# Attention output made transposed in the steady slots of an attention and ReGLU kernel

## The chip, the cores and the metric

The kernel runs on one core of a Trainium2 chip, as one launch. The metric is the device time of one execution in microseconds, as the median of several runs. A core has a matrix engine (PE, with its weight loads shown apart as PEld), a vector engine (DVE), a scalar engine (ACT), a general engine (POOL, here also the one that issues the loads), a synchronising engine (SP, here the one that issues DMA transposes), and 16 DMA engines that all queues share. Matmul results land in PSUM, which has eight banks, numbered 0 to 7 here. A bank's slice is 512 fp32 numbers on each of 128 partitions.

## What is computed

Inputs are q, k, v of shape (8 batches, 8 heads, 576 positions, 64) and three FFN matrices of 512x1536, 512x1536 and 1536x512. The result is 4608 x 512 in fp32.

```python
q_d = q.reshape(B, H, Sd, 4, D).mean(axis=3)          # k_d, v_d alike
out_up = np.repeat(sm_attn(q_d, k_d, v_d), 4, axis=2)  # softmax attention, 144 positions
mask = np.abs(pos[:, None] - pos[None, :]) < 4
scores = np.where(mask, scale * q @ k.T, -1e9)
out_local = softmax(scores) @ v                        # 7 keys for each query
x = (out_up + out_local).transpose(0, 2, 1, 3).reshape(4608, 512)
out = (np.maximum(x @ w_gate, 0.0) * (x @ w_val)) @ w_out
```

## The kernel before

**Tiling.** Two heads make a head pair, `hp` 0 to 31, four for each batch. The 576 positions are cut into 6 query blocks of 96, and each meets a window of 128 keys that starts three positions earlier; the band mask zeroes what lies outside. Pooled positions are two blocks of 72. The FFN goes over the 4608 tokens in 9 chunks of 512, and over d_ff in 12 blocks of 128 (`jj`).

**Steps of a head pair.** `emit_load` issues the loads on POOL with a cast to fp16: q and k (`qk16`, a ring of 7), v windows of 128 rows (`vw`, ring of 7, with a column of ones behind the 64 values), and from pair `NVP` = 9 on a second view of v (`v4`). q and k are transposed to `qkT`, for pairs below `NTP` = 9 by matmuls on PE (`emit_qkT_pe`, which also gives the sums of four), from 9 on by a DMA transpose on SP (`emit_qkT`) with `emit_pool` on DVE for the sums. The pooled v (`vd`, ring of 2) is made by six matmuls (`emit_vd`) for pairs below 9, and by two additions on POOL (`emit_vd_pool`) from 9 on. `emit_s1` makes scores and exponentials: `ee`, keys on partitions, and `ed` for the pooled part. `emit_s2` multiplies with `ee` and `ed` as the weights and v (65 columns, the last one gives the denominators) as moving data; it takes 8 matmuls for the pooled and 12 for the local part, and DVE divides (two reciprocals, two multiplications) into `xo`, which has queries on partitions. The FFN needs x with features on partitions, so `xo` is transposed: pairs below `NXP` = 9 on PE (`emit_x_pe`, 8 matmuls, which also repeat and add the pooled part), later pairs by a DMA transpose on SP (`emit_xoT`) and an addition on DVE (`emit_xadd`).

**FFN.** `emit_h` makes one `jj` block: 4 + 4 matmuls of 512 columns into a pair of banks, a ReLU on ACT, a product on DVE (`gT`). `emit_y` makes 128 rows of the result from the twelve `gT` of the chunk before, 12 matmuls, a copy on ACT and a store issued by ACT.

**Order.** Everything is written in order by hand: each engine runs its instructions as the code issues them. A fill of four pairs (with dummy matmuls, `emit_warm`) is followed by 36 slots; slot s makes a third of a quarter of chunk s//4, that is three `emit_h`, one `emit_y` of the chunk before (from slot 4 on), and the attention of a pair. `s2` of a pair comes one slot after its `s1`. Slots 5 and 6 (`EXTRA`) hold two pairs each, so pair 31 has its `s1` in slot 25. Slots 27 to 35 are FFN alone. Chunk c needs the pairs up to 4c+3.

**The load queue.** POOL issues the loads of pair hp+4 at the head of pair hp, just ahead of `emit_vd_pool(hp)`, and then waits in order. An issue waits until the ring slot is free, and until the load eight issues earlier has landed (eight semaphores take turns). `emit_vd_pool(hp)` waits for its `v4` and for `s2` of pair hp-2, which read the same `vd` buffer. What stands behind it on POOL waits with it.

Of the kernel before, what the change touches and what calls it, by code (L numbers as in the profile page):

```python
# [57 lines left out]
def kernel(  # L58
# [26 lines left out]
    NXP = 9  # L85
    NVP = 9
    EXTRA = (5, 6)
    B0 = 1

# [30 lines left out]
    ee = ring(2, [128, 2, S + 32], FP16, "ee_")  # L120
# [3 lines left out]
    xoT = ring(3, [128, NB + 2, 96], FP16, "xoT_")  # L124
    xT = keep.tile([128, NPB, NTOK], FP16, name="xT")
    ps = psum.tile([128, 8, 512], FP32, name="ps")

    nc.vector.memset(zero_sb, 0.0)
    for t in vw:
        nc.vector.memset(t[:, :, :, 64], 1.0)  # L130
# [16 lines left out]
    def emit_load(hp):  # L147
# [18 lines left out]
        if off == 0:  # L166
            nc.gpsimd.dma_start(
                t[:, 1:, 0:64], _dap(v, base + NQ * D, [[D, 128], [NQ * D, n - 1], [1, D]])
            )
            nc.gpsimd.dma_start(t[3:128, 0, 0:64], _dap(v, 0, [[D, 125], [1, D]]))  # L170
            nc.gpsimd.dma_start(t[0:3, 0, 0:64], _dap(v, 0, [[D, 3], [1, D]]))
        elif b == B - 1 and hp % NPB == NPB - 1:
            nc.gpsimd.dma_start(
                t[:, 0 : n - 1, 0:64], _dap(v, base, [[D, 128], [NQ * D, n - 1], [1, D]])
            )
            last = base + (n - 1) * NQ * D
            nc.gpsimd.dma_start(t[0:99, n - 1, 0:64], _dap(v, last, [[D, 99], [1, D]]))
            nc.gpsimd.dma_start(t[99:128, n - 1, 0:64], _dap(v, last + 67 * D, [[D, 29], [1, D]]))
        else:
            nc.gpsimd.dma_start(t[:, :, 0:64], _dap(v, base, [[D, 128], [NQ * D, n], [1, D]]))  # L180
# [20 lines left out]
    def emit_qkT_pe(hp, b0):  # L201
        r, r4, r2 = hp % NL, hp % 4, hp % 2
        sv = qk16[r].rearrange("p i (h j d) -> p i h j d", h=2, d=64)
        for n in range(2 * NB):
            lo = 120 * (n % 4)
            for hh in range(2):
                nc.tensor.matmul(
                    out=ps[64 * hh : 64 * hh + 64, b0 + n // 4, lo : lo + 120],
                    lhsT=sv[:, n // NB, hh, n % NB, :],
                    rhs=eyesum_sb,  # L210
                    start=True,
                    stop=True,
                )
        big = qkT[r4][:, 0 : 2 * S].rearrange("p (b n t) -> p b n t", b=3, n=4)
        sml = qkd[r2].rearrange("p i t -> p (i t)").rearrange("p (b n t) -> p b n t", b=3, n=4)
        tv = ps[:, b0 : b0 + 3, 0:480].rearrange("p b (n t) -> p b n t", n=4)
        nc.scalar.copy(out=big[:, 0], in_=tv[:, 0, :, 0:96])
        nc.scalar.copy(out=sml[:, 0], in_=tv[:, 0, :, 96:120])
        nc.vector.tensor_copy(out=sml[:, 1:3], in_=tv[:, 1:3, :, 96:120])
        nc.vector.tensor_copy(out=big[:, 1:3], in_=tv[:, 1:3, :, 0:96])  # L220

    def emit_vd_pool(hp):
        t, m, o = v4[hp % NV4], v2[hp % 2], vd[hp % 2]
        if hp < NVP + 2:
            nc.gpsimd.memset(o[:, :, :, 64], 4.0)
# [14 lines left out]
    def emit_vd(hp, loc):  # L240
        t = vw[hp % NL]
        o = halves(loc)
        for c in range(2):
            for sig in range(3):
                nc.tensor.matmul(
                    out=o[:, c, :, :],
                    lhsT=pool_sb[:, sig, :],
                    rhs=t[:, :, 3 * c + sig, :],
                    start=(sig == 0),
                    stop=(sig == 2),  # L250
                )
        nc.scalar.copy(out=vd[hp % 2], in_=o[0:72])

    def emit_s1(hp):
        r4, r2 = hp % 4, hp % 2
        p0 = 2
# [21 lines left out]
        for g in range(2):  # L278
            o = ee[r2][:, :, 288 * g : 288 * g + 288]
            nc.scalar.activation(  # L280
                out=o, in_=ps[:, p0 + 2 * g : p0 + 2 * g + 2, 0:288], func=AF.Exp, scale=scale
# [4 lines left out]
                in1=_sap(masks_sb, (0, 128), 288 * g, [[0, 2], [1, 288]]),  # L286
# [9 lines left out]
    def emit_s2(hp, loc, pu):  # L296
# [3 lines left out]
        for hh in range(2):  # L300
            for tcx in range(2):
                for c in range(2):
# [4 lines left out]
                        rhs=vd[r2][:, c, hh, :],  # L307
# [30 lines left out]
    def emit_xoT(hp):  # L338
        x = xo[hp % 3]
        nc.sync.dma_start_transpose(out=xoT[hp % 3], in_=x.rearrange("p j c -> p (j c)"))  # L340

    def emit_xadd(hp):
        b, kk = hp // NPB, hp % NPB
        r3 = hp % 3
        nc.vector.tensor_tensor(
            out=xT[:, kk, b * S : (b + 1) * S].rearrange("p (c t f) -> p c t f", c=2, f=4),
            in0=xoT[r3][:, 0:NB, :].rearrange("p j t -> p (j t)").rearrange(
                "p (c t f) -> p c t f", c=2, f=4
            ),
            in1=_sap(xoT[r3], (0, 128), NB * 96, [[96, 2], [1, 72], [0, 4]]),  # L350
# [3 lines left out]
    def emit_x_pe(hp, pp, on_dve=False):  # L354
# [16 lines left out]
        if on_dve:  # L371
            nc.vector.tensor_copy(out=o, in_=pair(pp)[:, :, 0:288])
        else:
            nc.scalar.copy(out=o, in_=pair(pp)[:, :, 0:288])
# [3 lines left out]
    def emit_h(c, jj, pp):  # L378
# [10 lines left out]
        r1 = ffn.tile([128, TCH], FP16, name="r1", tag="r1")  # L389
        nc.scalar.activation(out=r1, in_=h1, func=AF.Relu)  # L390
        gt = gpool.tile([128, TCH], FP16, name="gT", tag="gT")
        nc.vector.tensor_tensor(out=gt, in0=r1, in1=h2, op=ALU.mult)
        gts[c, jj] = gt
# [54 lines left out]
    def emit_fill(hp):  # L448
        emit_in(hp + 4)
        emit_s1(hp)  # L450
# [5 lines left out]
        if hp < LEAD - 1:  # L456
            emit_qkT_pe(hp + 1, 2)
# [5 lines left out]
    def emit_att_head(hp, loc=7, pu=2):  # L463
        emit_in(hp + 4)
        if hp - 1 < NP:
            emit_s2(hp - 1, loc, pu)
            if hp - 1 >= NXP:
                emit_xoT(hp - 1)
        if NVP <= hp < NP:
            emit_vd_pool(hp)  # L470
        if NTP <= hp + 3 < NP:
            emit_qkT(hp + 3)

    def emit_att_mid(hp):
        if NTP <= hp + 1 < NP:
            emit_pool(hp + 1)
        if hp < NP:
            emit_s1(hp)

    def emit_slot(s, hp):  # L480
        c, jj = s // 4, 3 * (s % 4)
        if s == 0:
            emit_in(hp + 4)
            emit_qkT_pe(hp, 2)
# [3 lines left out]
            emit_h(c, jj, 3)  # L488
            emit_s1(hp)
        elif s == 4:  # L490
            emit_att_head(hp)
            emit_y(c - 1, s % 4, 6)
            emit_x_pe(hp - 1, 1, on_dve=True)
            emit_h(c, jj, 0)
            emit_att_mid(hp)
        else:
            emit_att_head(hp)
            emit_h(c, jj, 0)
            if hp - 1 < NXP:
                emit_x_pe(hp - 1, 3)  # L500
            emit_att_mid(hp)
            if s > 4:
                emit_y(c - 1, s % 4, 6)
        if NXP <= hp - 2 < NP:
            emit_xadd(hp - 2)
        emit_h(c, jj + 1, 0)
        if hp < NVP:
            emit_vd(hp, 7)
        if hp + 1 < NTP:
            emit_qkT_pe(hp + 1, 4)  # L510
        if s in EXTRA:
# [53 lines left out]
```

## Time and profile before

| what | value |
|---|---|
| median of 3 runs | 388.07 us (385.64 to 393.62) |
| the profiled execution, whole | 386.8 us |
| its span, first to last instruction | 384.7 us |
| PE busy | 360.3 us |
| DVE, ACT, POOL busy | 220.8, 154.3, 188.3 us |
| HBM read, written | 48.03 MB, 9.44 MB |

A line of the page for a group of instructions gives the program's line, engine, operation, what is written and read, and the count; then busy time, the mean duration of one, and the idle time before them with what ended it. Matmuls overlap in the pipeline, so the duration of one (388 ns for 512 columns) is longer than the distance from one to the next (216 ns: eight in 1.73 us); distances are what counts, and a row of the timeline gives the start of a group, so the distance to the start of the next row is what the group takes.

The order of time has three parts: up to 30 us the fill, up to about 293 us slots with attention, and from there to 381 us FFN alone.

### The profile page before, as it was taken

How to read it: one execution, taken by the hardware profiler on the slowest of the kernel's cores; microseconds unless marked ns; L12 is line 12 of the kernel's file. 1: busy time of each engine (PE TensorE's matmuls, PEld its weight loads, DVE VectorE, ACT ScalarE, POOL GpSimd, SP SyncE). 2: the span in 40 equal slices, each digit the busy share in tenths (PEclk: the TensorE clock that was granted, in tenths of full speed). 3: DMA queues.
4: the chain of work that ended last, by engine and by line, in shares of the span. 5: the costliest groups of instructions: out<-in, count | busy, mean ns of one | idle time of the engine just before them, and what ended most of it. 6: DMA issues, size and time to landing. Idle time of an engine off the chain costs nothing.

```text
span 384.7 us, 7154 instructions
## 1 busy us (share of the span) xinstructions
PE 360.3 (94%) x2834; PEld 181.1 (47%) x2834; DVE 220.8 (57%) x384; ACT 154.3 (40%) x276; POOL 188.3 (49%) x233
## 2 busy tenths in 40 slices
PE   7999997997779998999969999999999999999995
PEld 3665553453435453445434545545444444444442
DVE  2676765466859775877835897877764322222210
ACT  1665563442524443444414444444443332333321
POOL 8856574899678637965378789911000000000000
PEclk9999999898989998999978999999999999999999
DMA  9999999999999999999999999954222100010012
GB/s 128 146 155 178 155 179 169 173 156 155 142 169 137 159 137 137 124 175 129 124 148 132 164 173 183 165 99 88 60 43 54 55 29 27 27 56 28 29 47 89
DMA packets 191282, 45.41 MB, mean 118 GB/s; under 512 B 174257, under 2 KB 186513, under 8 KB 191249
## 3 DMA queue, kind: packets, MB, share of 16 engines
q0 software_dynamic: 140272, 23.86, 100.9%
q1 hardware_dynamic: 45776, 11.66, 28.1%
q10 hardware_dynamic: 5200, 9.44, 8.5%
q8 instruction: 22, 0.36, 0.5%
q14 instruction: 12, 0.09, 0.1%
HBM read 48.03 MB, written 9.44 MB: 149 GB/s over the span
## 4 chain that ended last, share of the span: by engine, by line
PE 53%; DMA 31%; POOL 12%; issue 3%; DVE 0%; ACT 0%; POOLq 0%; DVEq 0%
PE ps L382 31%; PE ps L398 17%; DMA qk_5_80<-in_k_dram 7%; DMA wv_sb<-in_moe_w_val_dram 6%; DMA qk_3_78<-in_k_dram 5%; DMA vw_90<-in_v_dram 4%; DMA wo_sb<-in_moe_w_out_dram 3%; DMA qk_4_79<-in_q_dram 3%; DMA vw_91<-in_v_dram 2%; DMA vw_93<-in_v_dram 2%; PE ps L314 2%; POOL v_1_88 L226 1%; PE ps L304 1%; PE ps L260 1%; PE ps L271 1%
## 5 line engine op out<-in xcount | busy, mean ns | idle before, releaser
L382 PE MATMUL ps<-xT,wg_sb 128*128 128x512 f16 x432 | 114.2, 388 | 0.0
L382 PE MATMUL ps<-xT,wv_sb 128*128 128x512 f16 x432 | 113.7, 387 | 0.0
L398 PE MATMUL ps<-wo_sb,gT 128*128 128x512 f16 x432 | 100.1, 382 | 3.6 <-DMA wo_sb<-in_moe_w_out_dram 3.4
L382 PEld LDWEIGHTS <-wv_sb 128*128 128x128 f16 x432 | 43.0, 100 | 53.4 <-issue 4.1
L398 PEld LDWEIGHTS <-gT 128*128 128x128 f16 x432 | 40.7, 98 | 51.8 <-issue 4.9
L382 PEld LDWEIGHTS <-wg_sb 128*128 128x128 f16 x432 | 40.2, 99 | 44.1 <-issue 2.2
L406 ACT COPY y_sb<-ps 128x512 f32<-128x512 f32 x36 | 21.1, 587 | 70.8 <-PE ps L398 70.8
L280 ACT ACTIVATE ee_102<-ps 128x576 f16<-128x576 f32 x32 | 19.3, 649 | 12.9 <-PE ps L271 12.9
L280 ACT ACTIVATE ee_103<-ps 128x576 f16<-128x576 f32 x32 | 19.1, 649 | 11.5 <-PE ps L271 11.5
L283 DVE TENSOR_TENSOR ee_103<-ee_103,cst_sb 128x576 f16<-128x576 f16 x32 | 20.7, 676 | 3.0 <-ACT ee_103 L280 2.6
L283 DVE TENSOR_TENSOR ee_102<-ee_102,cst_sb 128x576 f16<-128x576 f16 x32 | 18.1, 599 | 2.8 <-ACT ee_102 L280 2.5
L227 POOL TENSOR_TENSOR vd_107<-v_1_88 72x256 f16<-72x256 f32 x12 | 9.1, 760 | 14.5 <-PE ps L304 13.7
L444 PE MATMUL ps<-zero_sb 128*128 128x512 f16 x44 | 14.3, 449 | 1.3 <-DVE vw_89 L130 1.3
L304 PE MATMUL ps<-vd_106,ed_104 72*128 72x65 f16 x128 | 6.6, 195 | 8.8 <-POOL vd_106 L227 8.8
L227 POOL TENSOR_TENSOR vd_106<-v_0_87 72x256 f16<-72x256 f32 x11 | 8.2, 745 | 8.0 <-PE ps L304 7.2
L304 PEld LDWEIGHTS <-ed_104 72*128 72x128 f16 x128 | 6.0, 98 | 12.8 <-issue 9.7
L322 DVE RECIPROCAL rd<-ps 72x4 f32<-72x4 f32 x32 | 5.5, 173 | 10.8 <-PE ps L304 10.8
L331 DVE TENSOR_TENSOR xo_108<-ps,ru 96x768 f16<-96x768 f32 x11 | 10.5, 954 | 0.4
L331 DVE TENSOR_TENSOR xo_109<-ps,ru 96x768 f16<-96x768 f32 x11 | 10.5, 954 | 0.4
L289 ACT ACTIVATE ed_105<-ps 72x576 f16<-72x576 f32 x16 | 10.3, 645 | 0.0
L289 ACT ACTIVATE ed_104<-ps 72x576 f16<-72x576 f32 x16 | 10.3, 644 | 0.0
L304 PE MATMUL ps<-vd_107,ed_105 72*128 72x65 f16 x128 | 6.7, 196 | 3.8 <-POOL vd_107 L227 3.8
(393 smaller groups left out, 560.9 us busy)
## 6 DMA issues: line engine op xcount, KB each, us to landing
out_dram<-y_sb ACTq DMA_DIRECT2D x35, 256.0 KB, 2.2
wg_sb<-in_moe_w_gate_dram POOLq DMA_DIRECT2D x4, 384.0 KB, 10.7
wv_sb<-in_moe_w_val_dram POOLq DMA_DIRECT2D x4, 384.0 KB, 11.0
wo_sb<-in_moe_w_out_dram POOLq DMA_DIRECT2D x4, 384.0 KB, 9.8
vw_90<-in_v_dram POOLq DMA_DIRECT2D x5, 192.0 KB, 10.5
vw_91<-in_v_dram POOLq DMA_DIRECT2D x5, 192.0 KB, 8.4
vw_92<-in_v_dram POOLq DMA_DIRECT2D x5, 192.0 KB, 11.2
vw_89<-in_v_dram POOLq DMA_DIRECT2D x4, 192.0 KB, 11.0
```

What stands on the lines that cost most here:

```text
L227: nc.gpsimd.tensor_tensor(out=o[:, :, :, 0:64].rearrange("p c h d -> p h c d"), in0=m[:, :, 0:64].rearrange("p (h c) d -> p h c d", h=2), ...
L280: nc.scalar.activation(out=o, in_=ps[:, p0 + 2 * g : p0 + 2 * g + 2, 0:288], func=AF.Exp, scale=scale)
L283: nc.vector.tensor_tensor(out=o, in0=o, in1=_sap(masks_sb, (0, 128), 288 * g, [[0, 2], [1, 288]]), op=ALU.mult,)
L289: nc.scalar.activation(out=ed[r2][:, :, 0 : 2 * SD].rearrange("p h (c t) -> p c h t", c=2), in_=ps[0:72, p0 : p0 + 4, 288:432].rearrange(" ...
L304: nc.tensor.matmul(out=od[:, hh, tcx, :], lhsT=ed[r2][:, hh, s0 : s0 + 128], rhs=vd[r2][:, c, hh, :], start=(c == 0), stop=(c == 1),)
L314: nc.tensor.matmul(out=u[:, hh, j, :], lhsT=ee[r2][:, hh, NQ * j : NQ * j + 128], rhs=vw[hp % NL][:, hh, j, :], start=True, stop=True,)
L322: nc.vector.reciprocal(out=rd, in_=od[0:72, :, :, 64])
L331: nc.vector.tensor_tensor(out=x[:, 0:NB, :].rearrange("p j (h d) -> p h j d", h=2), in0=u[0:96, :, :, 0:64], in1=_sap(ru, (0, 96), 0, [[NB ...
L382: nc.tensor.matmul(out=h, lhsT=w[:, kk, bass.ts(jj, 128)], rhs=xT[:, kk, c * TCH : (c + 1) * TCH], start=(kk == 0), stop=(kk == 3),)
L398: nc.tensor.matmul(out=y_ps, lhsT=gts[c, jj][:, bass.ts(ty, 128)], rhs=wo_sb[:, jj, :], start=(jj == 0), stop=(jj == NJJ - 1),)
L406: nc.scalar.copy(out=y_sb, in_=y_ps)
L444: nc.tensor.matmul(out=ps[:, 7, :], lhsT=zero_sb[:, 0:128], rhs=zero_sb[:, 128:640], start=True, stop=True)
```

## The change

From slot 1 on, `emit_s2t` takes the place of `emit_s2` (which stays for pairs 0 to 3, with `emit_x_pe`). It swaps the operands: v (64 columns) is the weights, `ee` and `ed` are moving data, so the result has features on partitions, head 0 of the pair on partitions 0 to 63 and head 1 on 64 to 127. The denominators come from matmuls with a matrix of ones (of fours for pairs whose `vd` is a sum) as weights, so that they stand on the same partitions, in banks 4 and 5; the products are in banks 2 and 3. ACT makes the reciprocal as exp(-ln(den)), DVE multiplies and adds the pooled part, repeated four times, straight into `xT`. `emit_xoT`, `emit_xadd` and all `x` transposes of pairs 4 to 31 go.

Key windows have 112 rows instead of 128. `EXTRA` goes, so each slot has one pair and pair 31 has its `s1` in slot 27. `vd` is made by `emit_vd` for pairs up to 12, is a ring of three, and `emit_vd_pool(hp + 1)` stands ahead of the loads of pair hp+4. `emit_h` hands back its ReLU and product as a function `gate`: those of the last block of a slot are issued in the next slot, between the Ln and the Exp. Banks move: the scores use banks 4 to 7, the three `emit_h` banks 0-1, 2-3 and 6-7, `emit_y` bank 1. One table load for the activation functions is asked for at the start.

```diff
-    NXP = 9
-    NVP = 9
-    EXTRA = (5, 6)
+    NVP = 13
     B0 = 1
+    WK = 112
...
-    vw = ring(NL, [128, 2, NB, 65], FP16, "vw_")
+    vw = ring(NL, [WK, 2, NB, 65], FP16, "vw_")
...
-    vd = ring(2, [72, 2, 2, 65], FP16, "vd_")
+    vd = ring(3, [72, 2, 2, 65], FP16, "vd_")
...
+    nc.scalar.preload_act_table_set("natural_log_exp_and_others")
...
-            nc.gpsimd.dma_start(t[:, :, 0:64], _dap(v, base, [[D, 128], [NQ * D, n], [1, D]]))
+            nc.gpsimd.dma_start(t[:, :, 0:64], _dap(v, base, [[D, WK], [NQ * D, n], [1, D]]))
...
-    def emit_xoT(hp):
...
+    def emit_s2t(hp, between):
+        r2, b, kk = hp % 2, hp // NPB, hp % NPB
+        e, d, one = ee[r2], ed[r2], 64 * (hp >= NVP)
+        for g in range(2):
+            for hh in range(2):
+                nc.tensor.matmul(
+                    out=ps[64 * hh : 64 * hh + 64, 4 + g, 0:288],
+                    lhsT=ones_sb[0:WK, 0:64],
+                    rhs=e[:, hh, 288 * g : 288 * g + 288],
...
+            for c in range(2):
+                for hh in range(2):
+                    nc.tensor.matmul(
+                        out=ps[64 * hh : 64 * hh + 64, 4 + g, 288:360],
+                        lhsT=ones_sb[0:72, one : one + 64],
+                        rhs=d[:, hh, c * SD + 72 * g : c * SD + 72 * g + 72],
...
+        for g in range(2):
+            for j in range(3):
+                for hh in range(2):
+                    nc.tensor.matmul(
+                        out=ps[64 * hh : 64 * hh + 64, 2 + g, NQ * j : NQ * j + NQ],
+                        lhsT=vw[hp % NL][:, hh, 3 * g + j, 0:64],
+                        rhs=e[:, hh, 288 * g + NQ * j : 288 * g + NQ * j + NQ],
...
+            for c in range(2):
+                for hh in range(2):
+                    nc.tensor.matmul(
+                        out=ps[64 * hh : 64 * hh + 64, 2 + g, 288:360],
+                        lhsT=vd[hp % 3][:, c, hh, 0:64],
+                        rhs=d[:, hh, c * SD + 72 * g : c * SD + 72 * g + 72],
...
+        r, x = rden[r2], xn[r2]
+        nc.scalar.activation(out=r, in_=ps[:, 4:6, 0:360], func=AF.Ln)
+        between()
+        nc.scalar.activation(out=r, in_=r, func=AF.Exp, scale=-1.0)
+        nc.vector.tensor_tensor(out=x, in0=ps[:, 2:4, 0:360], in1=r, op=ALU.mult)
         nc.vector.tensor_tensor(
             out=xT[:, kk, b * S : (b + 1) * S].rearrange("p (c t f) -> p c t f", c=2, f=4),
...
+            in0=x[:, :, 0:288].rearrange("p c (t f) -> p c t f", f=4),
+            in1=_sap(x, (0, 128), 288, [[360, 2], [1, 72], [0, 4]]),
             op=ALU.add,
...
+    def emit_slot(s, gate):
+        c, jj, hp = s // 4, 3 * (s % 4), s + LEAD
+        if NVP <= hp + 1 < NP:
+            emit_vd_pool(hp + 1)
         emit_in(hp + 4)
...
+        elif hp - 1 < NP:
+            emit_s2t(hp - 1, gate)
         else:
+            gate()
+        if s >= 4:
+            emit_y(c - 1, s % 4, 1)
+        else:
+            emit_h(c, jj, 0)()
+        if hp < NP:
+            emit_s1(hp, 4)
+        if NTP <= hp + 1 < NP:
+            emit_pool(hp + 1)
+        if s >= 4:
+            emit_h(c, jj, 0)()
+        emit_h(c, jj + 1, 1)()
         if hp < NVP:
-            emit_vd(hp, 7)
+            emit_vd(hp, 5)
         if hp + 1 < NTP:
...
+            emit_qkT_pe(hp + 1, 4, 0)
+        return emit_h(c, jj + 2, 3)
```

On ACT, at the start of slot 1, stood the rest of a transpose of q and k, the ReLUs of two FFN blocks (the last of slot 0 and the first of slot 1; `r_` is a ReLU's result), and the copy of `xT` from `emit_x_pe`:

```order
L218 CAST qkd_101<-ps 128x96
L390 ACTIVATE r_697<-ps 128x512
L390 ACTIVATE r_745<-ps 128x512
L374 CAST xT<-ps 128x576
L280 ACTIVATE ee_103<-ps 128x2x288 x2
L289 ACTIVATE ed_105<-ps 72x2x2x144
```

At the same place now, with Ln on line 382 and Exp on line 384 (`rden` holds the logarithm and then the reciprocal):

```order
L224 CAST qkd_101<-ps 128x96
L382 ACTIVATE rden_112<-ps 128x720
L428 ACTIVATE r_745<-ps 128x512
L384 ACTIVATE rden_112<-rden_112 128x720
L428 ACTIVATE r_760<-ps 128x512
L283 ACTIVATE ee_103<-ps 112x2x288 x2
L292 ACTIVATE ed_105<-ps 72x2x2x144
```

The ReLU of the last block of slot 0 has moved behind the Ln, two instructions of 720 columns came in, and the copy of `xT` went.

On POOL, behind the loads of pair 13 (`vw_95`, `v_3_85`), stood the pooled v of pair 9 (`vd_107`), and behind that the loads of pair 14:

```order
L180 DMA vw_95<-in_v_dram 128x12x64
L182 DMA v_3_85<-in_v_dram 72x4x256
L225 MEMSET vd_107 72x4
L226 ISA
L226 TENSOR_TENSOR v_1_88<-v_4_86 72x512
L227 TENSOR_TENSOR vd_107<-v_1_88 72x2x2x64
L159 DMA qk_0_75<-in_q_dram 96x6x64 x2
L159 DMA qk_0_75<-in_k_dram 96x6x64 x2
L180 DMA vw_89<-in_v_dram 128x12x64
```

Now the loads of pairs 14 and 15 follow at once, and the first pooled v on POOL is that of pair 13:

```order
L184 DMA vw_95<-in_v_dram 112x12x64
L186 DMA v_3_85<-in_v_dram 72x4x256
L163 DMA qk_0_75<-in_q_dram 96x6x64 x2
L163 DMA qk_0_75<-in_k_dram 96x6x64 x2
L184 DMA vw_89<-in_v_dram 112x12x64
L186 DMA v_4_86<-in_v_dram 72x4x256
L163 DMA qk_1_76<-in_q_dram 96x6x64 x2
L163 DMA qk_1_76<-in_k_dram 96x6x64 x2
L184 DMA vw_90<-in_v_dram 112x12x64
L186 DMA v_0_82<-in_v_dram 72x4x256
L230 ISA
L230 TENSOR_TENSOR v_1_88<-v_3_85 72x512
```

The additions for pairs 9 to 12 have left POOL for PE, and from there on a pooled v stands ahead of the loads of the pair three later, where it stood behind the loads of the pair four later.

More of the change, by code (lines that the diff above doesn't have):

```diff
@@ L251, in emit_vd, with emit_s1 @@
                 )
-        nc.scalar.copy(out=vd[hp % 2], in_=o[0:72])
-    def emit_s1(hp):
+        nc.scalar.copy(out=vd[hp % 3], in_=o[0:72])
+    def emit_s1(hp, p0):
         r4, r2 = hp % 4, hp % 2
-        p0 = 2
         for c in range(2):
@@ L280, in emit_s1 @@
             nc.scalar.activation(
-                out=o, in_=ps[:, p0 + 2 * g : p0 + 2 * g + 2, 0:288], func=AF.Exp, scale=scale
+                out=o, in_=ps[0:WK, p0 + 2 * g : p0 + 2 * g + 2, 0:288], func=AF.Exp, scale=scale
             )
@@ L352, in emit_xadd, with emit_x_pe @@
         )
-    def emit_x_pe(hp, pp, on_dve=False):
+    def emit_x_pe(hp, pp):
         b, kk = hp // NPB, hp % NPB
@@ L370, in emit_x_pe @@
         o = xT[:, kk, b * S : b * S + S].rearrange("p (g t) -> p g t", g=2)
[L371 to L374, printed above, removed]
+        nc.scalar.copy(out=o, in_=pair(pp)[:, :, 0:288])
     gts = {}
@@ L449, in emit_fill @@
         emit_in(hp + 4)
-        emit_s1(hp)
+        emit_s1(hp, 2)
         emit_vd(hp, 6)
```

132 lines of the change are left out of this document (49 added, 83 removed).

## The prediction

> **What bounds the kernel now.** I read the page first, its shares, slices, queues and chain.
>
> ```profile
> span 384.7 us, 7154 instructions
> PE 360.3 (94%) x2834; PEld 181.1 (47%) x2834; DVE 220.8 (57%) x384; ACT 154.3 (40%) x276; POOL 188.3 (49%) x233
> ...
> PEclk9999999898989998999978999999999999999999
> DMA  9999999999999999999999999954222100010012
> ...
> q0 software_dynamic: 140272, 23.86, 100.9%
> q1 hardware_dynamic: 45776, 11.66, 28.1%
> ...
> PE 53%; DMA 31%; POOL 12%; issue 3%; DVE 0%; ACT 0%; POOLq 0%; DVEq 0%
> ```
>
> PE is busy 94% of the span, yet the chain puts 43% on DMA and POOL: for the first 26 slices the DMA engines are full, and PE now and then waits for loads. Then I read who waits for whom, and the clock.
>
> ```profile
> PE ps L304 <- POOL vd_106 L227: 8.8, 3, 4.2
> ...
> PE ps L304 <- POOL vd_107 L227: 3.8, 1, 3.8
> ...
> PE ps L398 <- DMA wo_sb<-in_moe_w_out_dram: 3.4, 2, 2.3
> ...
> core 0: 384.7 us, clock 0.973
> ```
>
> PE waits 8.8 + 3.8 + 3.4 = 16.0 us: four times for the pooled v that POOL makes behind its loads, twice for the last FFN matrix. The clock costs more: (1 - 0.973) x 384.7 = 10.4 us of full-speed work. The timeline of PE shows that it is the same event.
>
> ```profile
> 108.48 0.40 PE L304 MATMUL ps<-vd_106,ed_104 72*128 72x65 f16 x8 [4.18 <-POOL vd_106 L227]
> ...
> 109.29 1.90 PE L382 MATMUL ps<-xT,wg_sb 128*128 128x512 f16 x4
> 110.98 1.66 PE L382 MATMUL ps<-xT,wv_sb 128*128 128x512 f16 x4
> 112.58 0.25 PE L260 MATMUL ps<-qkd_101 64*72 64x144 f16 x2
> ```
>
> After a wait of 4.18 us eight matmuls take 112.58 - 109.29 = 3.29 us, where the slot below needs 1.82. So waiting and its echo are 16.0 + 10.4 = 26.4 us of 384.7. An undisturbed slot with attention, on the timeline of PE:
>
> ```profile
> 237.73 0.41 PE L304 MATMUL ps<-vd_107,ed_105 72*128 72x65 f16 x8
> 237.98 0.55 PE L314 MATMUL ps<-vw_93,ee_103 128*128 128x65 f16 x12
> 238.37 1.02 PE L382 MATMUL ps<-xT,wg_sb 128*128 128x512 f16 x4
> ...
> 240.19 0.25 PE L260 MATMUL ps<-qkd_100 64*72 64x144 f16 x2
> ...
> 240.73 2.76 PE L398 MATMUL ps<-wo_sb,gT 128*128 128x512 f16 x12
> 243.33 1.03 PE L382 MATMUL ps<-xT,wg_sb 128*128 128x512 f16 x4
> ...
> 246.78 0.41 PE L304 MATMUL ps<-vd_106,ed_104 72*128 72x65 f16 x8
> ```
>
> It takes 246.78 - 237.73 = 9.05 us without a gap: s2 0.64 (to 238.37), one FFN block 1.82, s1 0.54, y 2.60, two blocks 3.45. So two limits alternate: loads early on, PE's own matmuls elsewhere.
>
> **Part 1: the waits.** How fast the loads go is read from a table by stage (bytes per us in the last column) and from the two issues of `vw` that frame pairs 14 and 25.
>
> ```profile
> 0.00:68.00 68.00, 61.27 (x758) 35.62 (x759) 40.19 (x97) 33.73 (x70) 44.53 (x56) 1.00 2.25 158
> 88.00:195.00 107.00, 97.70 (x761) 48.44 (x759) 77.09 (x121) 43.42 (x75) 72.53 (x89) 0.95 1.88 145
> ...
> 87.77 1.05 POOL L180 DMA_DIRECT2D vw_89<-in_v_dram  x1
> ...
> 195.02 1.03 POOL L180 DMA_DIRECT2D vw_93<-in_v_dram  x1 [1.80 <-DMA qk_3_78<-in_k_dram]
> ```
>
> Eleven pairs in 107.25 us is 9.75 us for one, slower than the slot of 9.05, and slots 5 and 6 ask for two pairs each: so the loads fall behind and PE waits. By the tiles' sizes in fp16 a pair moves 295 KB of q and k, 197 of vw, 147 of v4, 295 for the transpose of q and k, 197 for that of xo, and 262 of result: 1393 KB, and at 145 GB/s that is 9.6 us, which agrees. The change takes out 197 KB (the transpose of xo) and 16 of 128 rows of vw (25 KB): 1171 KB, 8.1 us, if bytes set the pace. The slot becomes longer (below, 9.65 us) and none holds two pairs. So loads gain 1.5 us a slot, and even at the old 9.75 they would lose only 0.1. POOL's new order lets the loads of pair h start after the s2t of pair h-6, in slot h-9; DVE needs the transpose in the middle of slot h-5, 4.4 slots or 42 us later, against 9.75 of load and the transpose behind it; that covers it. For the FFN matrix, the bytes ahead of it shrink by ten vw (250 KB) and one v4 (147): 0.4 MB, 2.5 us at 158 GB/s, so most of 3.4 us goes and I leave 1.4. Sum: -26.4 + 1.4 = **-25.0 us**. Bounds: 0 (all waits stay) and -26.4.
>
> **Part 2: work that moves on PE.** From the early slots:
>
> ```profile
> 38.93 0.29 PE L359 MATMUL ps<-cst_sb,xo_109 72*128 72x288 f16 x1
> ...
> 39.74 0.25 PE L260 MATMUL ps<-qkd_101 64*72 64x144 f16 x2
> ...
> 41.98 0.51 PE L245 MATMUL ps<-vw_94,cst_sb 128*128 128x130 f16 x6
> 42.42 0.82 PE L207 MATMUL ps<-cst_sb,qk_6_81 96*64 96x120 f16 x24
> 43.17 1.04 PE L382 MATMUL ps<-xT,wg_sb 128*128 128x512 f16 x4
> ```
>
> `emit_x_pe` takes 0.81 us (38.93 to 39.74) and goes for pairs 4 to 8: **-4.1 us**. `emit_vd` takes 0.44 (41.98 to 42.42) and comes for pairs 9 to 12: **+1.8**. That EXTRA goes moves two pairs to later slots and adds no work.
>
> **Part 3: s2t in place of s2, 28 times.** This decides. It has 32 matmuls of 64 weight columns in pairs, one for each half of the output partitions: 2 pairs of 288 columns, 6 of 96, 8 of 72. The nearest row is L207 above, which writes the two halves in the same manner: 24 matmuls in 0.75 us, 62.5 ns for a pair of 120 columns. One after the other at 512 columns in 216 ns they would need 24 x 51 = 1.2 us, so pairs do run side by side. I take 62.5 ns for each of the 14 small pairs (0.875), 288 columns at 0.42 ns plus 11 for the two large ones (0.265), and 0.1 for going from full width to half width (the six matmuls of 130 columns in L245 need 0.33 by columns, and 0.44 pass): 1.24 us, against 0.64 of s2. **+0.60 x 28 = +16.8 us.** Low end: side by side and by columns alone, (576 + 576 + 576) x 0.42 ns = 0.73 + 0.1, +0.19 x 28 = +5.3. High end: in turn, each at the price of a pair, 28 x 62.5 ns + 4 x 132 + 0.1 = 2.38, +1.74 x 28 = +48.7. I stay by L207, the only row with such halves.
>
> By the Trainium skill ("TensorE: Matmul & The Clock Gate", Part 3, "What overlaps and what doesn't") a weight load overlaps a running matmul only if their row groups differ, and both halves of s2t use the same rows; its section on LDWEIGHTS gives columns / 1.2 ns, 53 ns for 64. By that, an estimate, L207 would need 24 x (53 + 50) = 2.5 us. It shows 0.75, so the trace disagrees; by this rule one s2t would take 3456 x 0.42 + 32 x 53 ns = 3.1 us, and the time would be about 431 us. The Trainium skill, "TensorEngine Tiling (Array Packing)", "Restrictions", says that column tiling switches off the fast weight load, which the price of a small pair (62.5 ns against 50 by columns) does not contradict.
>
> **Part 4: the new chain on ACT and DVE.** Prices from the page and the timelines of DVE and ACT:
>
> ```profile
> L280 ACT ACTIVATE ee_102<-ps 128x576 f16<-128x576 f32 x32 | 19.3, 649 | 12.9 <-PE ps L271 12.9
> ...
> L331 DVE TENSOR_TENSOR xo_108<-ps,ru 96x768 f16<-96x768 f32 x11 | 10.5, 954 | 0.4
> ...
> 237.07 0.60 ACT L390 ACTIVATE r_3004<-ps 128x512 f16<-128x512 f32 x1 [0.99 <-PE ps L382]
> ...
> 243.93 0.75 DVE L345 TENSOR_TENSOR xT<-xoT_111 128x576 f16<-128x576 f16 x1
> ```
>
> Ln and Exp have 720 columns; from 512 in 0.60 and 576 in 0.65 some 0.78 us each. The product takes 0.90 (954 ns x 720/768), the addition 0.75 to 0.8. From the start of s2t: denominators done 0.8, Ln 1.6, ReLU 2.2, Exp 3.0, product 3.95, addition 4.8. In slots 1 to 3 the second FFN block wants banks 2 and 3, which the product reads, at 1.24 + 1.73 + 0.54 = 3.5: 0.5 of waiting, three times, **+1.5 us**. From slot 4 on y stands between, and that block comes at 6.1: no wait. Where a chunk begins (8 times) FFN needs the new x in the fourth matmul of its block, at 1.24 + 2.60 + 0.54 + 0.65 = 5.0, against 4.8; y's copy in bank 1 is as close in the seven last slots. I set **+0.8** for these; bounds 0 and 8 x 0.6. What leaves DVE and SP (0.17 + 0.42 + 0.22 and the transposes' issues) was hidden beside PE and gives nothing. ACT has 6 us of work in a slot, DVE 7, of 9.65.
>
> **Sum.** -25.0 - 4.1 + 1.8 + 16.8 + 1.5 + 0.8 = -8.2 us: span 376.5. The profiled execution was 386.8, 2.1 above its span, and 1.3 below the median of 388.07; with the same 2.1, 378.6, and I say **378 us**, 2.6% below the median. The slot is 9.05 + 0.60 = 9.65.
>
> **Rivals.**
> - *Halves in turn, by columns.* If only half of what L207 shows holds for s2t, whose halves read different moving data (in L207 both read the same), 3456 columns at 0.42 ns, 32 x 5 ns and 0.1 make 1.72 us: +1.08 x 28 = 30.2 in place of 16.8, **391 us**. For: that difference. Against: L207.
> - *Halves in turn, each waiting for its weights.* 2.38 us as above: +48.7, **410 us**, slower by over 5%. It decides against the change from +0.64 us above my 1.24, at 1.88 us for one s2t. L207 speaks against it. This is the mechanism to which the rule of the Trainium skill in part 3 points.
> - *The loads still come late.* If transposes of xo were not what held the loads up, or POOL's new order starts them too late, half of the waits and of the lower clock stay: +12, **390 us**. For: most of the DMA engines' time is q0's, which loses only 5% of its packets (32 pairs x 192 and 4 x 288 of 140272). Against: the slot is longer than the old pace and EXTRA is gone.
> - *A cheap s2t.* By columns alone 0.83 us: **366.5 us**. For: L304 and L314 run at 31 and 32 ns for 65 columns, near the column price. Against: the 12 ns that each pair of L207 takes beyond its columns.
>
> **How the numbers follow.** Mine 0.50 (its own range 371 to 385), cheap s2t 0.13, late loads 0.17, in turn by columns 0.12, in turn by weights 0.08. A measurement of this kernel can tell about 2% from no change, that is 380.3 and 395.8 us. Faster: three quarters of mine, all of the cheap one, a quarter of the late loads: 0.38 + 0.13 + 0.04 = 0.55. Slower: 0.08 and a little of each of the two at 390: 0.12. Same: 0.33. The range 366 to 392 leaves out the rival at 410 and the outer parts of the others, under 2 in 10.
>
> **What would show it.** No row of PE waiting for POOL or loads after 70 us, and a clock near 1.00, if part 1 holds. A steady slot of 9.65 us, and s2t 1.24 us from its first ones-matmul to y: this is the term I am least sure of. PE waits for DVE in slots 1 to 3 of some 0.5 us, and none at the starts of chunks. If DVE waits for the transposes of q and k instead, the loads came late; if s2t takes 1.7 or 2.4 us, one of the two rivals in turn holds.

## Result and profile after

The changed kernel took 374.75 us (median of 4 executions, 374.37 to 375.61) beside 388.56 for the kernel before on the same chip: 0.967 of its time, interval 0.961 to 0.973. The forecast was 378 us with a range of 366 to 392, faster. Ratios, here and below, leave out executions more than 1.5% above the fastest of their kernel, so they can differ a little from the quotient of two medians.

The page and the mean clock of the changed kernel's profiled execution (374.37 us, of which 372.6 are the span):

```profile
span 372.6 us, 7680 instructions
...
PE 359.6 (97%) x3154; PEld 179.2 (48%) x3154; DVE 196.0 (53%) x306; ACT 188.4 (51%) x332; POOL 173.5 (47%) x219
...
PEclk9999998999999999999999999999999999999999
DMA  9999999999999999999999999992000001000012
...
q0 software_dynamic: 132528, 22.48, 105.4%
q1 hardware_dynamic: 27376, 7.14, 16.3%
...
PE 79%; DMA 16%; POOL 2%; issue 1%; DVE 1%; ACT 0%; DVEq 0%; POOLq 0%
...
core 0: 372.6 us, clock 0.995
```

PE's busy time is about what it was (359.6 against 360.3 us) in a span that is 12.1 us shorter: 11.4 us of idle time went, and inside the busy time the 8.5 us that the low clock no longer costs about pay for the matmuls that were added. In the chain POOL fell from 12% to 2% and DMA from 31% to 16%. The DMA engines are still full for 27 slices: the loads still take most of the time with attention, but PE seldom waits for them. From the view of who waits for whom, the two waits of PE for a load (us in total, times, longest):

```profile
PE ps L418 <- DMA wv_sb<-in_moe_w_val_dram: 2.7, 1, 2.7
PE ps L438 <- DMA wo_sb<-in_moe_w_out_dram: 2.0, 1, 2.0
```

There is no row in which PE waits for POOL. PE's timeline (start, busy time, last column the wait ahead of it) shows both waits, and the echo of the first in the clock:

```profile
57.69 1.04 PE L418 MATMUL ps<-xT,wv_sb 128*128 128x512 f16 x4 [2.67 <-DMA wv_sb<-in_moe_w_val_dram]
...
59.18 1.89 PE L418 MATMUL ps<-xT,wg_sb 128*128 128x512 f16 x4
60.86 1.83 PE L418 MATMUL ps<-xT,wv_sb 128*128 128x512 f16 x4
...
70.56 0.81 PE L438 MATMUL ps<-wo_sb,gT 128*128 128x512 f16 x3 [1.99 <-DMA wo_sb<-in_moe_w_out_dram]
```

Both are for FFN matrices, before 73 us. From 59.18 to 60.86 four matmuls of 512 columns take 1.68 us, where 0.87 is usual. The lower clock costs (1 - 0.995) x 372.6 = 1.9 us in all, where it was 10.4.

A steady slot with `s2t`, on the same timeline:

```profile
207.07 1.03 PE L418 MATMUL ps<-xT,wg_sb 128*128 128x512 f16 x4
...
208.80 1.03 PE L418 MATMUL ps<-xT,wg_sb 128*128 128x512 f16 x4
...
210.62 0.31 PE L346 MATMUL ps<-ee_102,ones_sb 112*64 112x288 f16 x2
210.77 0.23 PE L355 MATMUL ps<-ed_104,ones_sb 72*64 72x72 f16 x4
210.84 0.29 PE L346 MATMUL ps<-ee_102,ones_sb 112*64 112x288 f16 x2
210.96 0.23 PE L355 MATMUL ps<-ed_104,ones_sb 72*64 72x72 f16 x4
211.03 0.29 PE L365 MATMUL ps<-ee_102,vw_90 112*64 112x96 f16 x6
211.16 0.23 PE L374 MATMUL ps<-ed_104,vd_107 72*64 72x72 f16 x4
211.23 0.29 PE L365 MATMUL ps<-ee_102,vw_90 112*64 112x96 f16 x6
211.35 0.23 PE L374 MATMUL ps<-ed_104,vd_107 72*64 72x72 f16 x4
211.52 2.76 PE L438 MATMUL ps<-wo_sb,gT 128*128 128x512 f16 x12
...
220.00 0.31 PE L346 MATMUL ps<-ee_103,ones_sb 112*64 112x288 f16 x2
```

The slot is 220.00 - 210.62 = 9.38 us, 0.33 more than 9.05; 9.65 was forecast. `s2t` takes 211.52 - 210.62 = 0.90, and the block ahead of it 1.82 in place of 1.73 (the block before that, 207.07 to 208.80): 0.99 with the entry, where 1.24 was forecast. The starts say why. A row of six 96-column matmuls, three pairs of halves, lasts from 211.03 to 211.16: 43 ns for a pair. Four of 72 columns, two pairs, take 70 ns: 35 for a pair. Both are columns x 0.42 ns to within 5 ns.

The terms of the sum, in us of span (384.7 to 372.6):

| term | forecast | measured | from |
|---|---|---|---|
| waits for loads and POOL, and low clock | -25.0 | -19.8 | 16.0 to 4.7, 10.4 to 1.9 |
| `emit_x_pe` goes | -4.1 | -4.1 | no such rows |
| `emit_vd` on PE for four pairs more | +1.8 | +1.4 | four of 0.35 |
| `s2t` in place of `s2`, 28 times | +16.8 | +9.2 | slot 9.05 to 9.38 |
| bank waits in slots 1 to 3 | +1.5 | +0.5 | two of 0.26 |
| starts of chunks and the rest | +0.8 | +0.7 | what remains |
| sum | -8.2 | -12.1 | |

### The profile page after: what moved, and what is told of

It is laid out like the page before. It is cut to its first block, busy times and chain, and to the rows that moved or that the text cites. A ratio compares the mean times of both kernels' runs of the same rounds, so it can differ in the third digit from the quotient of the medians.

```text
span 372.6 us, 7680 instructions
## 1 busy us (share of the span) xinstructions
PE 359.6 (97%) x3154; PEld 179.2 (48%) x3154; DVE 196.0 (53%) x306; ACT 188.4 (51%) x332; POOL 173.5 (47%) x219
## 4 chain that ended last, share of the span: by engine, by line
PE 79%; DMA 16%; POOL 2%; issue 1%; DVE 1%; ACT 0%; DVEq 0%; POOLq 0%
PE ps L418 45%; PE ps L438 25%; DMA wv_sb<-in_moe_w_val_dram 7%; DMA wo_sb<-in_moe_w_out_dram 3%; DMA qk_5_80<-in_k_dram 3%; DMA qk_3_78<-in_k_dram 2%; PE ps L346 2%; PE ps L365 2%; PE ps L274 2%; PE ps L263 2%; PE ps L374 1%; PE ps L355 1%; POOL qk_0_75 L156 1%; PE ps L249 0%; POOL qk_2_77 L156 0%
## 5 line engine op out<-in xcount | busy, mean ns | idle before, releaser
L418 PE MATMUL ps<-xT,wv_sb 128*128 128x512 f16 x432 | 111.7, 381 | 2.7 <-DMA wv_sb<-in_moe_w_val_dram 2.7
L418 PE MATMUL ps<-xT,wg_sb 128*128 128x512 f16 x432 | 112.2, 382 | 1.1 <-ACT xT L410 0.5
L382 ACT ACTIVATE rden_113<-ps 128x720 f32<-128x720 f32 x14 | 10.8, 771 | 33.0 <-PE ps L355 33.0
L382 ACT ACTIVATE rden_112<-ps 128x720 f32<-128x720 f32 x14 | 10.8, 771 | 32.4 <-PE ps L355 32.4
L283 ACT ACTIVATE ee_103<-ps 112x576 f16<-112x576 f32 x32 | 19.1, 648 | 11.3 <-PE ps L274 6.1
L286 DVE TENSOR_TENSOR ee_102<-ee_102,cst_sb 112x576 f16<-112x576 f16 x32 | 15.2, 488 | 18.1 <-ACT ee_102 L283 17.2
L286 DVE TENSOR_TENSOR ee_103<-ee_103,cst_sb 112x576 f16<-112x576 f16 x32 | 16.9, 539 | 14.3 <-ACT ee_103 L283 13.4
L283 ACT ACTIVATE ee_102<-ps 112x576 f16<-112x576 f32 x32 | 19.1, 648 | 8.9 <-ACT y_sb L446 5.1
L385 DVE TENSOR_TENSOR xn_115<-ps,rden_113 128x720 f16<-128x720 f32 x14 | 12.7, 908 | 0.0
L385 DVE TENSOR_TENSOR xn_114<-ps,rden_112 128x720 f16<-128x720 f32 x14 | 12.7, 907 | 0.0
L346 PEld LDWEIGHTS <-ones_sb 112*64 112x64 f16 x112 | 6.2, 107 | 11.9 <-issue 11.9
L355 PEld LDWEIGHTS <-ones_sb 72*64 72x64 f16 x224 | 11.4, 111 | 0.6
L384 ACT ACTIVATE rden_112<-rden_112 128x720 f32<-128x720 f32 x14 | 11.3, 805 | 0.0
L384 ACT ACTIVATE rden_113<-rden_113 128x720 f32<-128x720 f32 x14 | 11.3, 805 | 0.0
L386 DVE TENSOR_TENSOR xT<-xn_115 128x576 f16<-128x576 f16 x14 | 10.6, 759 | 0.5
L386 DVE TENSOR_TENSOR xT<-xn_114 128x576 f16<-128x576 f16 x14 | 10.6, 758 | 0.5
## 6 DMA issues: line engine op xcount, KB each, us to landing
wg_sb<-in_moe_w_gate_dram POOLq DMA_DIRECT2D x4, 384.0 KB, 11.4
wv_sb<-in_moe_w_val_dram POOLq DMA_DIRECT2D x4, 384.0 KB, 12.1
```

What stands on the lines that cost most here:

```text
L283: nc.scalar.activation(out=o, in_=ps[0:WK, p0 + 2 * g : p0 + 2 * g + 2, 0:288], func=AF.Exp, scale=scale)
L286: nc.vector.tensor_tensor(out=o, in0=o, in1=_sap(masks_sb, (0, WK), 288 * g, [[0, 2], [1, 288]]), op=ALU.mult,)
L346: nc.tensor.matmul(out=ps[64 * hh : 64 * hh + 64, 4 + g, 0:288], lhsT=ones_sb[0:WK, 0:64], rhs=e[:, hh, 288 * g : 288 * g + 288], start=Tr ...
L355: nc.tensor.matmul(out=ps[64 * hh : 64 * hh + 64, 4 + g, 288:360], lhsT=ones_sb[0:72, one : one + 64], rhs=d[:, hh, c * SD + 72 * g : c * ...
L382: nc.scalar.activation(out=r, in_=ps[:, 4:6, 0:360], func=AF.Ln)
L384: nc.scalar.activation(out=r, in_=r, func=AF.Exp, scale=-1.0)
```

## The experiments

Twelve runs of ten kernels in three batches, each timed beside the kernel before (387.92, 390.76 and 388.82 us in the three). Ratios are to the kernel before of the same batch. Executions of one changed kernel lie up to 7 us apart, those of the kernel before up to 12, and those of `b_poolorder` 15, so where waits matter the profile of one execution is read beside the median.

### What ended the waits

The kernel before, with POOL's order changed alone (one more `vd` buffer, the pooled v ahead of the loads):

```diff
-    vd = ring(2, [72, 2, 2, 65], FP16, "vd_")
+    vd = ring(3, [72, 2, 2, 65], FP16, "vd_")
...
+        if NVP <= hp + 1 < NP:
+            emit_vd_pool(hp + 1)
         emit_in(hp + 4)
...
-        if NVP <= hp < NP:
-            emit_vd_pool(hp)
```

> The kernel before, with only the order on POOL of the changed one: vd is a ring of three, and the pooled v of pair hp+1 is made ahead of the loads of pair hp+4. Theory L (the loads' pace made PE wait: 9.75 us for a pair against a slot of 9.05, and two double slots): nothing comes earlier, PE waits in the same places or DVE waits for the transposes of q and k instead, 382 to 390 us. Rival P (the pooled v stood behind load issues on POOL that themselves wait for other loads): the four waits of 12.6 us and most of the lower clock behind them go, 364 to 370 us.

The profiled execution took 368.41 us, the three timed ones 377.50, 378.82 and 383.22; they lie 15 us apart, and no ratio is given. Where PE waited for a load or POOL in the profiled one:

```profile
PE ps L398 <- DMA wo_sb<-in_moe_w_out_dram: 3.1, 2, 2.0
```

There is no wait for POOL at all: the order, with its third buffer, can end these waits alone. That is what rival P expected (364 to 370 us). Of the other three executions two lie between its range and that of theory L and one in that of theory L; they have lower clocks (0.982 to 0.991, against 0.995), so PE probably waited in them, which no profile shows. How much the order is worth stays open.

This execution also tells what the loads can do. The issues of `vw` for pairs 14 and 25, the same two from which the prediction took its pace:

```profile
91.20 1.05 POOL L180 DMA_DIRECT2D vw<-in_v_dram  x1
...
184.57 1.03 POOL L180 DMA_DIRECT2D vw<-in_v_dram  x1 [1.09 <-DMA qk<-in_k_dram]
```

Eleven pairs in 93.37 us is 8.49 us for one, at 157 GB/s, with every byte of the kernel before. So 9.75 us was not a limit that these bytes set; with the same bytes, it came with the old order on POOL.

The kernel before, with the 23 transposes of `xo` for pairs 9 to 31 left out. The addition then reads zeros, so the attention output of these pairs is missing in the result:

```diff
-        nc.sync.dma_start_transpose(out=xoT[hp % 3], in_=x.rearrange("p j c -> p (j c)"))
+        return x
...
+        for t in xoT:
+            nc.gpsimd.memset(t, 0.0)
```

> The kernel before without the DMA transposes of xo (the addition then reads zeros, so pairs 9 to 31 are left out of the result). If 197 of 1393 KB for a pair are what holds the loads up: pace 8.2 us against 9.05, the waits in the second half (1.9 and 3.8 us) go and those near 90 and 105 us shrink, 366 to 376 us. If the double slots and POOL's order make the waits whatever the pace: 380 to 387 us.

It took 375.23 us, 0.967 (0.962 to 0.972). On PE's timeline two of the four waits for POOL are left:

```profile
94.10 0.40 PE L304 MATMUL ps<-vd,ed 72*128 72x65 f16 x8 [3.04 <-POOL vd L227]
...
107.46 0.40 PE L304 MATMUL ps<-vd,ed 72*128 72x65 f16 x8 [0.63 <-POOL vd L227]
```

12.6 us have become 3.7, with the old order on POOL, and none comes after 108 us. So leaving out the transposes alone takes most of them too. The waits for the last FFN matrix did not shrink with them: 4.8 us, where the kernel before had 3.4.

The changed kernel with everything put back that acts on the loads: 128 rows, the old order on POOL with two `vd` buffers, POOL's sums from pair 9 on, and transposes of `xo` into buffers that nobody reads. What is left of the change is one pair per slot, and `s2t` with what belongs to it:

```diff
-    NVP = 13
+    NVP = 9
...
-    WK = 112
+    WK = 128
...
-    vd = ring(3, [72, 2, 2, 65], FP16, "vd_")
+    vd = ring(2, [72, 2, 2, 65], FP16, "vd_")
+    xoT = ring(3, [128, NB + 2, 96], FP16, "xoT_")
...
-        if NVP <= hp + 1 < NP:
-            emit_vd_pool(hp + 1)
         emit_in(hp + 4)
+        if NVP <= hp < NP:
+            emit_vd_pool(hp)
+        if 9 <= hp - 1 < NP:
+            nc.sync.dma_start_transpose(
+                out=xoT[hp % 3], in_=xo[hp % 3].rearrange("p j c -> p (j c)")
+            )
```

> The changed kernel with everything on the side of the loads undone at once: 128 rows, pooled v on POOL from pair 9 on, vd a ring of two with the old order on POOL, and the transposes of xo on SP (unread). What stays of the change are the slots of one pair each and s2t. If the pace decides (slots of 9.4 us and no double slots, against 9.6 to 9.75 us of loads for a pair): no wait for POOL, 369 to 376 us. If bytes or POOL's order are needed: waits for POOL come back, two to four of 2 to 4 us with half speed behind, 380 to 390 us.

375.72 us, 0.967 (0.960 to 0.974), where the changed kernel itself took 372.49 in the same batch. Its waits for loads and POOL:

```profile
PE ps L439 <- DMA wo_sb<-in_moe_w_out_dram: 3.3, 2, 2.6
PE ps L375 <- POOL vd L232: 3.0, 3, 1.2
```

With the old bytes and the old order, waits for POOL are 3.0 us and not 12.6: slots of one pair, 9.38 us long, take most of them as well.

Two parts were put back singly in the changed kernel: the old order on POOL with two `vd` buffers (as above), and the transposes of `xo`, unread (as above).

> The changed kernel, with the old order on POOL: vd is a ring of two, and the pooled v of pair hp is made behind the loads of pair hp+4. Theory L: 374 to 377 us, since the loads have slack in any order. Rival P: PE waits for POOL again, two to four times 2 to 4 us with half speed behind, 380 to 390 us.

> The changed kernel, with the 23 DMA transposes of xo put back on SP (nobody reads what they write, and what they transpose is old data). Theory L by bytes: the pace goes back from 8.1 to 9.6 us for a pair against a slot of 9.38, so some waits come back between 90 and 250 us, 377 to 383 us. Rival P, or pace with slack enough: 374 to 376 us.

372.22 us (370.70 to 377.82), 0.960 (0.952 to 0.968), and 373.55 us (370.03 to 376.15), 0.958 (0.947 to 0.969): by these ratios neither is slower than the changed kernel (0.959 to 0.967 in the three batches that hold it). Neither has a wait for POOL, though the first was profiled in its longest execution. By stage, for 90 to 250 us (length, busy time of PE, PEld, DVE, ACT and POOL with counts, clock, DMA share, GB/s), the changed kernel:

```profile
90.00:250.00 160.00, 159.71 (x1443) 79.20 (x1442) 99.66 (x135) 90.81 (x156) 113.02 (x143) 1.00 1.62 134
```

and with the transposes back:

```profile
90.00:250.00 160.00, 159.25 (x1438) 79.02 (x1437) 106.86 (x134) 89.42 (x154) 114.78 (x139) 1.00 1.88 153
```

The loads carry 153 GB/s instead of 134, and PE is busy throughout in both. So no one of three things made the waits for POOL by itself: the fast and double slots, the transposes of `xo`, and sums queued on POOL behind load issues. Taking away the transposes left 3.7 of the 12.6 us, longer single slots left 3.0, and the new order left none in the one execution profiled; with the others gone, putting the old order or the transposes back costs nothing that shows.

### What sets the waits that remain

The changed kernel with windows of 128 rows, in load and computation (`WK = 128`, and the tail load of a row's last block 67 rows further on), was run twice, the second time beside the unchanged changed kernel, `after_c`:

> The changed kernel with key windows of 128 rows as before. If rows are bytes only: 25 KB more for each pair, 0.25 MB ahead of the last FFN matrix, so the two waits for FFN weights near 55 and 69 us grow by up to 1.6 us, 374 to 378 us. If loads of 112 rows are slower for their shape (the stage from 40 to 60 us moved 143 GB/s, before 169): these waits shrink, 370 to 373 us.

> The changed kernel with windows of 128 rows, beside the changed kernel on the same chip. If 112 rows slow the early loads by their shape, it is 3 to 5 us below after_c in each round; if the earlier difference was only that of two chips or executions, the two agree within 1.5 us.

> The changed kernel once more, beside the three others of this call, as their yardstick. Theory L and rival P alike: 370 to 376 us.

369.67 us, 0.956 (0.949 to 0.963), and 368.76 us, 0.952 (0.946 to 0.958), against 372.49 for `after_c`, 0.959 (0.951 to 0.966). So 128 rows, with 14% more bytes of `vw`, are not slower but 3.7 us faster in the median of the same batch, though the fastest execution of `after_c`, 368.74 us, lies among theirs. To part the load from the computation, v was loaded with 128 rows, and the matmuls took 112 of them:

```diff
+    WL = 128
...
-    vw = ring(NL, [WK, 2, NB, 65], FP16, "vw_")
+    vw = ring(NL, [WL, 2, NB, 65], FP16, "vw_")
...
-            nc.gpsimd.dma_start(t[:, :, 0:64], _dap(v, base, [[D, WK], [NQ * D, n], [1, D]]))
+            nc.gpsimd.dma_start(t[:, :, 0:64], _dap(v, base, [[D, WL], [NQ * D, n], [1, D]]))
...
-                        lhsT=vw[hp % NL][:, hh, 3 * g + j, 0:64],
+                        lhsT=vw[hp % NL][0:WK, hh, 3 * g + j, 0:64],
```

> The changed kernel, but v windows are loaded with 128 rows; all that is computed stays at 112 rows. If the shape of the load costs the 3 to 4 us between after_c and a_wk128_c: 368 to 370 us, with some 160 GB/s in the first 60 us against some 149, and no wait for FFN weights above 2 us in all. If computing with 112 rows costs it: as after_d.

> The changed kernel, as the yardstick of this call: 369 to 376 us.

369.08 us (368.04 to 369.40), 0.952 (0.947 to 0.957), against 374.41 (370.06 to 376.58), 0.964 (0.955 to 0.973), for the changed kernel in the same batch: no execution of one reaches into those of the other. The first 60 us by stage, the changed kernel (`after_d`):

```profile
0.00:60.00 60.00, 52.45 (x688) 30.26 (x690) 34.48 (x83) 32.35 (x65) 37.03 (x48) 1.00 2.59 143
```

and with the 128-row loads:

```profile
0.00:60.00 60.00, 55.28 (x734) 32.29 (x735) 36.32 (x87) 35.40 (x72) 42.17 (x53) 1.00 2.20 161
```

The loads move 161 GB/s in place of 143, more than the bytes added, and PE gets through 734 matmuls in this stage instead of 688. The narrower load is what costs; computing with 112 rows or with 128 takes the same time (369.08 against 368.76 and 369.67). But the narrow load is not slow in every execution. `a_xot` loads 112 rows too, and its added transposes start at 79 us; its first 60 us, profiled in an execution of 371.05 us:

```profile
0.00:60.00 60.00, 55.53 (x726) 32.17 (x728) 36.01 (x86) 34.85 (x71) 41.36 (x53) 1.00 2.24 157
```

Why loads of 112 rows are slower in most executions, and not in this one, is open. The two versions with 128-row loads are the fastest measured, 0.952 to 0.956 of the time before, and faster than the changed kernel too.

With 128 rows, and the sums of pairs 9 to 12 back on POOL (`NVP = 9`):

> The best so far, a_wk128_c, with the pooled v of pairs 9 to 12 on POOL again: four times 0.35 us of PE go, but four more loads of 147 KB stand in the early queue, 1 us each at 150 GB/s. If the early loads have no slack: 369 to 372 us, waits for FFN weights grow. If they have: 367 to 368 us.

372.60 us (371.60 to 375.33), 0.962 (0.956 to 0.969), 3.5 above `a_load128`. In its waits POOL does not appear, but the last FFN matrix does:

```profile
PE ps L438 <- DMA wo_sb<-in_moe_w_out_dram: 4.5, 3, 1.6
```

In `a_load128` these waits are 1.4 us. The sums themselves are not the reason: on POOL the first of them comes after the waits. What stands ahead of the FFN matrix is the second load of v (`v4`) of pair 9:

```profile
50.95 0.75 POOL L186 DMA_DIRECT2D v<-in_v_dram  x1
52.18 0.76 POOL L465 DMA_DIRECT2D wo_sb<-in_moe_w_out_dram  x1 [0.47 <-DMA wg_sb<-in_moe_w_gate_dram]
...
74.00 1.17 POOL L230 TENSOR_TENSOR v<-v 72x512 f32<-72x512 f16 x1
```

The first issue of the matrix comes at 52.18 us, in `a_load128` at 50.12. So `emit_vd` for pairs 9 to 12 costs PE 1.4 us and spares the early queue the loads of `v4`, which buys more than it costs; how much of it this one load makes was not tested.

### The price of s2t

All 32 matmuls of `s2t` twice, with the same results:

```diff
-        for g in range(2):
-            for hh in range(2):
+        for _ in range(2):
+            for g in range(2):
+                for hh in range(2):
```

> The changed kernel with the 32 matmuls of s2t issued twice, to the same banks. What one repetition adds has no entry and no exit. If pairs of small matmuls cost 62.5 ns each, as the prediction had it: 14 x 62.5 + 265 ns = 1.14 us for each s2t, 28 times, 404 us. If pairs go by their columns and the rest of s2t is a fixed cost: 0.73 to 0.80 us, 393 to 396 us.

391.18 us, 1.012 (1.005 to 1.018). On PE's timeline, the start, the start of the repetition, the y behind it and the next slot:

```profile
210.91 0.31 PE L347 MATMUL ps<-ee,ones_sb 112*64 112x288 f16 x2
...
211.71 0.29 PE L347 MATMUL ps<-ee,ones_sb 112*64 112x288 f16 x2
...
212.58 2.76 PE L439 MATMUL ps<-wo_sb,gT 128*128 128x512 f16 x12
...
221.06 0.31 PE L347 MATMUL ps<-ee,ones_sb 112*64 112x288 f16 x2
```

The slot is 10.15 us, 0.77 above 9.38. By columns alone the 16 pairs need 0.73, by the price that I took from L207 they need 0.875 + 0.265 = 1.14. So a repetition costs the columns, and what the first run has beyond it, 0.90 + 0.09 - 0.77 = 0.22, is paid once. 28 x 0.77 = 21.6 us would put the kernel at 396; the medians differ by only 16.8 and the profiled spans by 18.3, and 391.18 lies below the 393 that was expected at least. Smaller early waits and a higher clock in this execution (3.1 us and 0.999, against 3.8 and 0.995) make up 2.2 of the 3.3 us that are missing from the spans; the rest stays open.

## Why the prediction was right, and where its sizes were off

**Part 1, the waits: right that they end, wrong in the reason given first, and 5 us too large.** The change ended the waits for POOL: none is left, PE waits for nothing loaded but the FFN matrices, and for no load after 73 us. But the step "slower than the slot of 9.05 [...] so the loads fall behind and PE waits" does not hold: `b_poolorder` moved the same bytes at 8.49 us a pair, with the same slots and no wait for POOL. I read the 9.75 us as what the loads can do, and took it as confirmed by 1393 KB at 145 GB/s; but these 145 GB/s were measured over the same stretch, so they could only give the same pace again. The credit came out all the same, because the change also held the new order on POOL, which I had looked at only for whether it starts the loads soon enough.

The step that made the size wrong is "the bytes ahead of it shrink": of the 3.4 us for the FFN matrix I left 1.4, counting ten narrower `vw` as 250 KB saved. The 128-row runs show that the narrower loads lost time instead: 147 GB/s in the first 60 us of the changed kernel (143 in `after_d`), and not the 158 that I carried over from the kernel before. 4.7 us of waits stayed, with 1.9 of lower clock. With 128-row loads 1.4 us of waiting is left in `a_load128`, 1.7 and 0.5 in the two runs that also compute with 128 rows; that 1.4 is also what I had set down is chance.

I ascribed the end of the waits to bytes, order and `EXTRA` together. The runs show that each alone can end most of the waits for POOL or all of them, so their shares do not add. What the order alone is worth in time stays open.

**Part 2, moved work: right.** -4.1 as forecast. A new `emit_vd` takes 0.35 us where a full-width block follows,

```profile
75.27 0.51 PE L249 MATMUL ps<-vw_90,cst_sb 112*128 112x130 f16 x6
75.62 1.03 PE L418 MATMUL ps<-xT,wg_sb 128*128 128x512 f16 x4
```

which is nearly its columns (0.33); the 0.44 that I read from the kernel before had L207's half-width matmuls behind it, and its last 0.1 belonged to that change of width.

**Part 3, s2t: the term that was mis-sized, +16.8 forecast and +9.2 measured.** The step that failed is "I take 62.5 ns for each of the 14 small pairs". L207 has 24 matmuls and 12 of its 62.5 ns are not in the columns; I read them as a price of each pair, when most of them are a cost of the group: 0.75 - 12 x 0.050 = 0.15 us once. The trace of the kernel before already had it, in the row of the last pair and the one behind it:

```profile
43.02 0.22 PE L207 MATMUL ps<-cst_sb,qk_6_81 96*64 96x120 f16 x2
43.17 0.39 PE L382 MATMUL ps<-xT,wg_sb 128*128 128x512 f16 x1
```

From the last pair to the next group pass 0.15 us, 0.10 more than its columns; the eleven pairs from 42.42 to 43.02 take 55 ns each, the start of the group included. For `s2t` the doubled run settles it: 0.77 for a repetition against 1.14 by my price. The group costs its columns and about 0.22 around them, 0.09 of it in the block ahead. The rival of a cheap `s2t` (0.83) was nearer to 0.99 than I was.

The doubled run also ends both rivals in turn: 1.7 us by columns and 2.4 us by weights against 0.99. The Trainium skill's rule ("TensorE: Matmul & The Clock Gate", Part 3, "What overlaps and what doesn't") that a weight load overlaps a matmul only where row groups differ does not hold for these halves, which share their rows: the estimate by it, 3.1 us, stands against 0.99. The Trainium skill, "TensorEngine Tiling (Array Packing)", "Key Properties", says that a change of tiling mode drains TensorE; the trace agrees, with about 0.09 us at the entry of `s2t` and, in the rows of L207, 0.10 at the exit.

**Part 4, the chain: each price right to some hundredths, the end half a microsecond earlier.** The timelines of ACT and DVE in the changed kernel's slot at 210.62:

```profile
211.24 0.77 ACT L382 ACTIVATE rden_112<-ps 128x720 f32<-128x720 f32 x1 [2.50 <-PE ps L355]
211.90 0.59 ACT L428 ACTIVATE r_2948<-ps 128x512 f16<-128x512 f32 x1
212.38 0.81 ACT L384 ACTIVATE rden_112<-rden_112 128x720 f32<-128x720 f32 x1
...
213.22 0.91 DVE L385 TENSOR_TENSOR xn_114<-ps,rden_112 128x720 f16<-128x720 f32 x1
214.16 0.76 DVE L386 TENSOR_TENSOR xT<-xn_114 128x576 f16<-128x576 f16 x1
```

Ln was set at 0.78, the ReLU at 0.60, Exp at 0.78, the product at 0.90, the addition at 0.75 to 0.8. The chain ends 214.92 - 210.62 = 4.3 us after the start, before 4.8, and the waits for banks are two of 0.26 (three in `a_load128`) in place of three of 0.5; the first:

```profile
39.94 1.02 PE L418 MATMUL ps<-xT,wg_sb 128*128 128x512 f16 x4 [0.26 <-DVE xn_114 L385]
```

**The late-loads rival** put half of waits and low clock, 12 us, as staying. 6.6 of 26.4 stayed, for FFN matrices and not for the pairs' loads.

**The sum.** 7.6 too much for `s2t` and 5.2 too much credit for the waits went opposite ways; with 1.5 us of small terms the span came out 3.9 below the forecast's 376.5. The direction rested on the waits; the nearness owes something to two errors that offset each other.

## What to carry to other kernels

Price small matmuls in pairs of halves by their columns plus a fixed cost at the ends of the group, and tell the two apart by comparing groups of different counts, or by doing the group twice; dividing one group's time by its count turns an end cost into a price of each. Where waits come from several pressures at once, remove them one at a time before adding up shares: here each of three took away most of the waits. A pace measured while the loads themselves stood waiting is not what they can do. And a load that moves fewer bytes with another number of rows is a new transfer whose pace has to be measured.

## What the runs showed of the hardware

The loads of 112 rows were slower than those of 128 in most executions: 143 to 149 GB/s over the first 60 us in five of six profiled, 157 in `a_xot`, against 156 to 162 in the five profiled with 128 rows and the changed kernel's order of slots; 374.41 against 369.08 us for the kernel in one batch. The Trainium skill ("DMA: Bandwidth & Descriptors", "Why a DMA increments its semaphore by 16 and not by 1") lets a transfer use the largest count of engines up to 16 that divides the outer dimension on both sides; 112 is 16 x 7, so by that rule both widths use all 16, and it gives no reason for the difference. No run here shows which part of the transfer is slower.

The execution that was profiled can differ from others of the same kernel by 15 us (368.41 to 383.22 in `b_poolorder`), and by only 1.4 us (368.04 to 369.40) in `a_load128`. What differs between executions of the first was not profiled.
